# The first set of a second attention in pieces of 4, 4 and 8 tiles, two units spread by TensorE, other load order, new list of the first stages

## The chip, the cores and the metric

The kernel runs on one core of a Trainium2 chip. The metric is the device time of one execution in microseconds (us): the median of three runs of the kernel before is 1481.76 us (1481.65 to 1482.52). The core has five engines with a program of their own each: PE (TensorE, matrix products), DVE (VectorE), ACT (ScalarE), POOL (GpSimd) and SP (SyncE, which here only issues transfers). They wait for each other through semaphores; 16 DMA engines move data.

## The reference

```python
def _attn_ref(x, inducing):           # x: 4 x 12416 x 128, inducing: 32 x 128
    ...
    def mab(q, kv):
        s = scale * (q @ kv.transpose(0, 2, 1))
        s = s - s.max(-1, keepdims=True)
        a = np.exp(s)
        a /= a.sum(-1, keepdims=True) + 1e-09
        return a @ kv
    h = mab(I, x)
    return mab(x, h)

def _moe_ref(x, w_gate, w_val, w_out, rms_g):   # 49664 x 128, d_ff 1536
    rms = np.sqrt(np.mean(x * x, axis=-1, keepdims=True) + 1e-06)
    xn = x / rms * rms_g
    g = xn @ w_gate
    silu = g * (1.0 / (1.0 + np.exp(-g)))
    val = xn @ w_val
    return silu * val @ w_out
```

For each of four batches, 32 inducing rows attend to all 12416 rows of x and give h (32 x 128); then each row of x attends to h. A feed-forward layer with an RMS norm and a SwiGLU follows, row by row. The three weights arrive as 64-bit floats.

## The kernel before

**Tiling.** A batch has 97 tiles of 128 rows, in seven sets: five of 16 tiles, one of 15 and one of 2 (`per`). For the second attention a set is cut into four units, one for each group of 32 partitions (the last set is one unit), so a batch has 25 units, 100 in all. A unit has 512, 480 or 256 rows of x as columns. The output of the second attention is never formed: a unit's normalised weights `a` (32 values for each row, in a high and a low half) are multiplied on TensorE with stacked products of h and the weights (`stacks`, one for gate and one for value). For each of the 12 blocks of 128 hidden columns a unit passes through `gate`, `silu`, `value`, `times_value` (line 751, the product of silu and value on DVE) and a projection by w_out. The projection is either plain (kind P: one 32-bit product, line 807) or split into two or three parts that ACT, POOL and DVE prepare (kinds S and D: two products at lines 795 and 796 and a third at line 807). The list `sorts` names the kind of each of the 1200 blocks.

**Order.** Nothing is scheduled by the chip: every engine runs its instructions in the order in which the kernel issues them. The order is written out by hand in two strings. `ORDER` is the list of the first stages (`first()`), and `program` with `taken` is that of everything after; `banks`, `workers`, `outputs`, `holders` and `picks` say which buffer each step gets.

**First stages.** For batch 0, TensorE turns each set's rows (`t`, line 908; copied out by ACT `a` or DVE `v`, line 914), multiplies them with the inducing rows (`s`), and DVE takes scores and row maxima (`m`, line 920). The sets are in three groups (0, 1, 2), (3, 4), (5, 6), each with its own maximum (`own`, `mB`, `nb`). ACT takes exponentials (`e`, line 945), DVE turns them (`r`, line 354), TensorE sums (`h`, line 953). At the end the three groups are weighed (`by`, line 966), added by `turn_h` (line 972), and `hT` (line 977) is h turned. Then the second attention's first set is done in two halves of 8 tiles, 256 columns each, steps with a `z` in their name: scores (`sc`, line 994), transpose (`T`), row maximum (`rm`), subtraction (`sub`, DVE), exponential (`ex`), transpose (`ta`), product with the gram matrix of h (`sq`), product and sum (`zm`, `sm`), clamp (`mm`), power -1/2 on POOL (`rt`, line 1032), multiplication (`ap`), transpose (`tb`), and the two halves (`hi` on ACT, `lo` on DVE). TensorE spreads unit 0 to all partitions (`sd`, line 1054), ACT copies it (`cp`); units 1 and 2 are gathered by four transfers each on SP (`gather`, line 647).

Between these steps the list puts the rounding of the 64-bit weights, one chunk of 512 columns at a time: `p`, `u`, `g`, `l` on DVE (lines 226, 239, 248, 254), `P`, `U` mostly on ACT (lines 204, 206), `j` on POOL (line 260), `q` on SP. A chunk's raw words are fetched by `fetch_raw` (line 178), five of them ahead, the others when a place comes free. `st` and `low` make the first stacks (lines 485, 488, 492). `w` with a number is that many products of the identity with itself, whose result is not used.

**Loads.** `load_rows` issues the sets on SP in the order 0 to 6: one transfer for each of sets 0 to 4 (line 104), two for set 5, four for set 6 (line 100). One raw chunk is fetched after set 3 and four after set 6. In set 0 the row of partition p and tile t is 16p+t, so its four units interleave with the output rows by partition groups (`of`).

## Time and profile before

| What | us |
|---|---|
| median of three runs | 1481.76 |
| the profiled execution | 1481.53 |
| its span | 1479.7 |
| TensorE busy in the span | 1467.6 |
| first gate starts (after the span's start) | 46.99 |

The profile is one execution. Its views give, for each engine, busy time, the groups of instructions by line, the idle time ahead of an instruction with what ended it (in brackets, behind an arrow), the chain of waits that ended last, and the time from the issue of a transfer to its landing. In the rows of a timeline the first number is the start after the span's start and the second the length of that row's instructions together; x4 says how many instructions one row holds.

### The profile page before, as it was taken

To read this page: it belongs to the slowest core of one execution; us is meant where nothing else is said; L and a number is where in the kernel's file an instruction comes from. 1 tells how busy PE (TensorE), PEld (TensorE's weight loads), DVE (VectorE), ACT (ScalarE), POOL (GpSimd) and SP (SyncE) were. 2 spreads that over 40 slices of the span, in tenths; PEclk is the share of its full clock that TensorE was granted. 3 is DMA by queue.
4 is the path that set the end of the run, shared out by engine and by line. 5 is a ranking of instruction groups with operands and counts; after the bars stand their busy time and mean duration, and the time that the engine had idled before them with its cause. 6 is when DMAs were issued, how large, how long until landed. Compare 5 with 4: busy or idle time off the path is not lost.

```text
span 1479.7 us, 26001 instructions
## 1 busy us (share of the span) xinstructions
PE 1467.6 (99%) x7286; PEld 1102.4 (74%) x7286; DVE 1420.0 (96%) x2469; ACT 1309.5 (88%) x2605; POOL 1378.8 (93%) x1204
## 2 busy tenths in 40 slices
PE   9999999999999999999999999999999999999998
PEld 6566777877777777787777777777778777787787
DVE  6999998999999999999999999899999999999997
ACT  5798889889988898988998988988998989899997
POOL 1499998999999999999999999999989999999998
PEclk9999999999999999999999999999999999999999
DMA  7694324448453231465656321264232122222122
GB/s 286 129 127 94 68 40 92 88 116 128 78 102 73 42 70 32 94 136 103 116 89 117 56 44 29 43 136 107 58 63 45 33 38 38 42 38 42 36 43 35
DMA packets 391712, 116.28 MB, mean 79 GB/s; under 512 B 365584, under 2 KB 370704, under 8 KB 389008
## 3 DMA queue, kind: packets, MB, share of 16 engines
q1 hardware_dynamic: 390976, 114.55, 39.8%
q8 instruction: 58, 0.95, 0.3%
q14 instruction: 86, 0.70, 0.2%
q10 hardware_dynamic: 592, 0.08, 0.0%
HBM read 53.95 MB, written 27.00 MB: 55 GB/s over the span
## 4 chain that ended last, share of the span: by engine, by line
PE 94%; DVE 2%; DMA 1%; issue 1%; ACT 1%; POOL 0%; SPq 0%; DVEq 0%; ACTq 0%; POOLq 0%
PE gv L807 31%; PE gv L709 17%; PE gv L737 17%; PE gv L795 12%; PE gv L796 12%; PE gv L316 3%; PE gv L369 1%; PE gv L908 1%; DMA xn<-in_x_dram 1%; DVE u L751 0%; PE gv L569 0%; DMA xT<-in_x_dram 0%; PE gv L463 0%; DVE o L239 0%; DVE we L248 0%
## 5 line engine op out<-in xcount | busy, mean ns | idle before, releaser
L719 ACT ACTIVATE silu<-gv 128x512 f32<-128x512 f32 (+2 forms) x1200 | 671.4, 592 | 74.4 <-PE gv L709 55.9
L815 POOL TENSOR_TENSOR xn<-xn,xn 128x512 fp32r<-128x512 f32 (+2 forms) x486 | 605.0, 1264 | 15.5 <-PE gv L796 14.0
L709 PE MATMUL gv<-a,sg 128*128 128x512 f32 (+2 forms) x1188 | 482.1, 431 | 0.6 <-DMA a<-lo 0.6
L737 PE MATMUL gv<-a,sv 128*128 128x512 f32 (+2 forms) x1188 | 449.4, 411 | 0.3 <-ACT silu L719 0.2
L751 DVE TENSOR_TENSOR gv<-silu,gv 128x512 f32<-128x512 f32 (+2 forms) x643 | 422.1, 676 | 10.2 <-PE gv L737 5.0
L764 ACT ACTIVATE xn<-gv 128x512 fp32r<-128x512 f32 (+1 forms) x629 | 370.0, 598 | 32.9 <-DVE gv L751 27.0
L751 DVE TENSOR_TENSOR u<-silu,gv 128x512 f32<-128x512 f32 (+2 forms) x557 | 354.5, 652 | 12.2 <-PE gv L737 5.3
L807 PE MATMUL gv<-u,wo 128*128 128x512 f32 (+2 forms) x724 | 353.5, 573 | 1.1 <-DVE u L751 1.0
L770 DVE SCALAR_TENSOR_TENSOR xn<-xn,gv 128x512 fp32r<-128x512 f32 (+1 forms) x516 | 337.4, 664 | 8.9 <-ACT xn L764 6.2
L709 PEld LDWEIGHTS gv<-a,sg 128*128 128x128 f32 x1188 | 223.3, 189 | 106.6 <-issue 32.4
L737 PEld LDWEIGHTS gv<-a,sv 128*128 128x128 f32 x1188 | 222.9, 189 | 86.9 <-issue 21.4
L815 POOL TENSOR_TENSOR xn<-xn 128x512 fp32r<-128x512 f32 (+1 forms) x204 | 255.3, 1257 | 7.0 <-PE gv L796 4.0
L777 POOL TENSOR_TENSOR xn<-u,xn 128x512 fp32r<-128x512 f32 (+2 forms) x174 | 218.2, 1260 | 15.7 <-ACT xn L761 15.2
L815 POOL TENSOR_TENSOR u<-xn,u 128x512 fp32r<-128x512 f32 (+2 forms) x133 | 167.9, 1271 | 2.1 <-PE gv L796 1.9
L795 PE MATMUL gv<-xn,xn 128*128 128x512 f32 (+1 forms) x441 | 169.7, 385 | 0.0
L807 PEld LDWEIGHTS gv<-u,wo 128*128 128x128 f32 x724 | 134.9, 190 | 27.9 <-issue 10.9
L795 PE MATMUL gv<-xn,more 128*128 128x512 f32 (+2 forms) x355 | 137.6, 388 | 0.0
L796 PE MATMUL gv<-xn,xn 128*128 128x512 f32 (+2 forms) x363 | 135.9, 374 | 0.0
L807 PE MATMUL gv<-xn,xn 128*128 128x512 f32 (+2 forms) x363 | 135.0, 383 | 0.5 <-POOL xn L815 0.3
L783 ACT ACTIVATE xn<-xn 128x512 fp32r<-128x512 f32 (+2 forms) x194 | 122.0, 633 | 10.8 <-POOL xn L777 9.2
L761 ACT ACTIVATE xn<-u 128x512 fp32r<-128x512 f32 (+2 forms) x194 | 121.0, 625 | 6.9 <-DVE u L751 6.1
L807 PE MATMUL gv<-xn,more 128*128 128x512 f32 (+2 forms) x311 | 118.8, 396 | 0.0
(223 smaller groups left out, 1787.8 us busy)
## 6 DMA issues: line engine op xcount, KB each, us to landing
out_dram<-o SPq DMA_DIRECT2D x320, 64.0 KB, 2.0
xT<-in_x_dram SPq DMA_DIRECT2D x60, 256.0 KB, 4.6
xn<-in_x_dram SPq DMA_DIRECT2D x60, 256.0 KB, 5.8
a<-hi SPq DMA_DIRECT2D x156, 64.0 KB, 2.0
a<-lo SPq DMA_DIRECT2D x156, 64.0 KB, 2.0
xn<-in_x_dram SPq DMA_DIRECT2D x5, 1024.0 KB, 9.6
xn<-w SPq DMA_DIRECT2D x18, 256.0 KB, 4.2
out_dram<-o SPq DMA_DIRECT2D x64, 60.0 KB, 2.0
```

Of the source, the lines that this page charges most:

```text
L709: nc.tensor.matmul(g[:, 0:T], stacks[b][0][:, ts(j, P)], halves_in_turn(one["a"][:, 0:T]), start=True, stop=True)
L719: nc.scalar.activation(sl[:, 0:T], gates.pop(n)[:, 0:T], AF.Silu)
L737: nc.tensor.matmul(v[:, 0:T], stacks[b][1][:, ts(j, P)], halves_in_turn(one["a"][:, 0:T]), start=True, stop=True)
L751: nc.vector.tensor_tensor(out=to, in0=sl[:, 0:T], in1=v[:, 0:T], op=ALU.mult)
L764: nc.scalar.activation(hi, t["u"], AF.Copy, scale=-(1.0 - 2.0 ** -13) * 2.0 ** -12)
L770: nc.vector.scalar_tensor_tensor(out=t["lo"], in0=t["hi"].bitcast(F32), scalar=4096.0, in1=t["u"], op0=ALU.mult, op1=ALU.add)
L777: nc.gpsimd.tensor_tensor(out=t["lo"], in0=t["u"], in1=t["hi"].bitcast(F32), op=ALU.subtract)
L783: nc.scalar.activation(t["hi"], t["hi"].bitcast(F32), AF.Copy, scale=-(2.0 ** -12))
L795: nc.tensor.matmul(to, weight_of(0, j), halves_in_turn(t["hi"]), start=not one["q"], stop=False)
L796: nc.tensor.matmul(to, weight_of(1, j), halves_in_turn(t["lo"]), start=False, stop=last)
L807: nc.tensor.matmul(to.rearrange("p (n h) -> p h n", h=2) if step2 else to, lhsT, rhs, start=one["left"] == NJ, stop=one["left"] == 1)
L815: nc.gpsimd.tensor_tensor(out=t["lo"], in0=t["hi"].bitcast(F32), in1=t["lo"].bitcast(F32), op=ALU.add)
```

## The change

The load order becomes sets 1, 2, 0, 3 to 6, then all five raw chunks. Set 1 comes in three transfers, set 2 in two, set 5 in two as before. Set 0 is placed in another way, in 12 transfers: tiles 0 to 3 hold rows 0 to 511, tiles 4 to 7 rows 512 to 1023, tiles 8 to 15 the rest, so that unit 0 is piece 0, unit 1 is piece 1, and units 2 and 3 lie in piece 2.

In the list of the first stages, the second attention's set 0 goes in pieces of 4, 4 and 8 tiles. Pieces 0 and 1 run through to the end; TensorE spreads both of their units with eight selecting matrices (`sel`, four quarters by two halves), eight products for a unit, and two copies on ACT for each unit take them out. Piece 2 is taken up to its exponential; its other ten steps stand in `program`. Units 2 and 3 are gathered by eight transfers each. The row maximum is subtracted on POOL for pieces 0 and 1, and `ap1` and `lo1` go to POOL. The share of a group is multiplied in as soon as its sum is there (`hs`), 1/l goes into `fold` (`fr`), and `turn_h` is three separate steps. The copies, warm-ups and rounding steps are put on other engines and into another order, and `low1` stands in the list. The sums of group 1 have a bank of their own.

`banks`, `workers`, `outputs`, `holders`, `sorts`, `picks`, `program` and `taken` are new. `sorts` has 366 blocks of kind P, 191 D and 643 S, where before it had 362, 195 and 643.

```diff
+    PIECES = {1: (slice(0, 4), slice(4, 8), slice(8, 16)), 2: (slice(0, 8), slice(8, 16)), full - 1: (slice(0, 8), slice(8, 15))}
...
-            for part in (slice(0, 8), slice(8, n)) if s == full - 1 else (slice(0, n),):
+            if not s:
+                for k in range(4):
+                    q, tiles, first = (4, slice(4 * k, 4 * k + 4), 0) if k < 2 else (2, slice(8, 16), 2 * (k - 2))
+                    d = xrows[ds(512 * k, 512), :].rearrange("(i q t) c -> q i t c", i=m, q=q)
+                    for e in range(q):
+                        nc.sync.dma_start(out=t[ts(first + e, m), tiles, :], in_=d[e])
+                return
+            for part in PIECES.get(s, (slice(0, n),)):
                 nc.sync.dma_start(out=t[:, part, :], in_=d[:, part, :])
...
+        if (b, s) == (0, 0):
+            a = moving[b, u] = xnp.tile([P, 512], F32R, name="xn1") if u == 2 else astk.tile([P, 512], F32R, name="a")
+            for k, half in enumerate((hi, lo, hi, lo)):
+                for e in range(2):
+                    nc.sync.dma_start(out=a[ts(k, m), ts(e, w // 2)].bitcast(F32),
+                                      in_=half[ts(2 * (u - 2) + e, m), w // 2:w].bitcast(F32))
+            return
...
-    for s in range(NS):
+    for s in (1, 2, 0, *range(3, NS)):
         load_rows(0, s)
-        for _ in range(1 if s == 3 else 4 if s == NS - 1 else 0):
+        for _ in range(5 if s == NS - 1 else 0):
             fetch_raw(*unread.pop(0))
...
-        open w3 t02 t00 t03 v00 t01 a01 a03 v02 t10 a10 t12 t13 s0 a12 a13 t11 t20 t21 a20 t23 m0 a23 t22 a22 a21 v11
-        s1 t32 m1 t30 s2 a32 t33 t31 p00 P00 v30 u00 m2 own0 g00 Uv00 mB0 t40 l00 j00 q00 t42 nb0 a31 a33 t41 a40 v42 e0 t43
...
-        r6 h6 l10 j10 q10 by0 by1 by2 P20 g20 u11 turn_h hT sc0z sc1z U20 l20 j20 q20 T0z rm0z sub0z ex0z T1z gram ta0z w7 sq0z rm1z
-        sub1z ex1z zm0z ta1z sm0z st1 sq1z mm0z zm1z P11 silu sm1z mm1z rt0z rt1z p01 st0 U11 ap0z low0 tb0z
-        ap1z hi0z tb1z lo0z w12 sd0z hi1z P01 cp0z lo1z w1 sd1z u01 cp1z w3 gather1 gather2
+        open w4 t10 t11 c11A w2 t13 c13A c10V t12 t20 t21 c21V c12A s1 m1 c20A t22 t23 t00 c00A c22V t01 t02 t03 c23V
+        c01V c02A s2 c03A s0 m2 m0 t31 own0 t30 c31A c30V t33 mB0 nb0 c33V t32 c32V e2 t42 c42A r2 t40 t43 c40V t41 c41V
+        e0 t50 c43A s3 r0 s4 m3 e1 ls0 c50A p00 m4 t60 c60A p10 t53 c53A own1 t52 c52A r1 t51 mB1 nb1 u10 c51A s6 m6 p20
+        h0 u00 e3 r3 s5 m5 e4 ls1 h1 own2 mB2 P00A g00 nb2 U00A l00 j00 least P20A e6 h3 r4 e5 ls2 r6 h2 share shared h4
+        P10A hs0A r5 tl spl u20 p11 h5 U10A rl g20 hs1A g10 frA th0 l10 U20A h6 hs2A l20 P11A th1 th2 hgV hTA w2 sc0 sqh
+        gc sc1 j10 T0 rm0 sub0G sc2 st0 ex0 T1 rm1 sub1G T2 ta0 q00 j20 rm2 ex1 sq0 ta1 zm0 sm0 mm0V w1 sq1 stc0 q10 st1
+        stc1 rt0 zm1 sm1 mm1V sub2V ex2 ap0V tb0 low0 hi0 rt1 ap1G lo0V w6 sdh0 sdl0 silu p01 tb1 u01 hi1 cpa0A u11 sdm0
+        cpb0A low1 P01A lo1G sdh1 sdm1 U11V cpb1A q20 sdl1 cpa1A U01V
...
+        PARTS = (slice(0, 4), slice(4, 8), slice(8, 16))
...
+        def select(u, q, kind):
+            half = split_of[0, 0][kind][:, both(u)[0]]
+            T.matmul(at["spread", u, q // 2][:, ts(q % 2, P)], sel[q, kind], half, start=not kind, stop=bool(kind))
+
+        def spread(u):
+            for k in range(2):
+                at["spread", u, k] = bank()
+                select(u, 2 * k, 0)
+
+        def spread_rest(u, k):
+            select(u, 2 * k, 1)
+            select(u, 2 * k + 1, 0)
+            select(u, 2 * k + 1, 1)
...
+            for name, (engine, step) in piece.items():
+                add(0, engine, step, call=(), key=("piece", 0, name))
```

In the list, a letter behind a name is the engine (A for ACT, V for DVE, G for POOL); `sdh` is `spread`, `sdl` and `sdm` are `spread_rest` for the two halves of a unit's columns.

More of the change, by code (lines that the diff above doesn't have):

```diff
@@ L1051, in spread @@
-        def spread(k):
-            ps = at["spread", k] = bank()[:, 0:HT * m]
-            for n, half in enumerate(split_of[0, 0]):
-                T.matmul(ps, sel[:, n, :, :].rearrange("p k m -> p (k m)"), half[:, both(k)[0]], start=not n, stop=bool(n))
-        def spread_copy(k):
-            if not k:
-                moving[0, 0] = astk.tile([P, 512], F32R, name="a")
-            S.copy(out=moving[0, 0][:, both(k)[0]], in_=at.pop(("spread", k)))
+                split_of[0, 0] = [halves.tile([P, 512], F32R, name="hi")]
@@ L1065, in first, with choice @@
         do = {"open": f["open_"], "least": least_of, "share": shares, "shared": shared,
-              "fold": f["fold_l"], "turn_h": turn_h, "hT": copy_h, "gram": lambda: (f["square_h"](), f["copy_gram"]()), "silu": table}
+              "tl": f["total_l"], "spl": f["spread_l"], "rl": f["inverse_l"], "sqh": f["square_h"], "gc": f["copy_gram"],
+              "silu": table}
+        def choice(name, step):
+            for letter, by in engine.items():
+                do[name + letter] = lambda by=by: step(by)
+        choice("fr", fold_r)
+        choice("hT", copy_h)
+        choice("hg", scale_h)
         for n in range(1, 40):
@@ L1096, in first @@
+        for u in range(2):
+            do[f"sdh{u}"] = lambda u=u: spread(u)
+            for k, name in enumerate(("sdl", "sdm")):
+                do[f"{name}{u}"] = lambda u=u, k=k: spread_rest(u, k)
+            for k, name in enumerate(("cpa", "cpb")):
+                choice(f"{name}{u}", lambda by, u=u, k=k: spread_copy(by, u, k))
         for name in ORDER.split():
             do[name]()
+        assert not turns and not works and not outs
+        for engine_name, name, step, *args in (("DVE", "ta", turn_a), ("PE", "sq", square), ("DVE", "zm", times),
+                                               ("DVE", "sm", total), ("POOL", "mm", clamp, G), ("POOL", "rt", root),
+                                               ("POOL", "ap", apply, G), ("DVE", "tb", turn_b), ("ACT", "hi", upper),
+                                               ("POOL", "lo", lower, G)):
+            piece[name] = (engine_name, lambda step=step, args=args: step(*args, 2))
```

609 lines of the change are left out of this document (315 added, 294 removed), and 62 rows, old and new, of the table taken.

## The prediction

> **What bounds the kernel now.** I read the page first, then busy time by stretch, then TensorE's waits, then the chain and the queues of the first 50 us.
>
> ```profile
> PE 1467.6 (99%) x7286; PEld 1102.4 (74%) x7286; DVE 1420.0 (96%) x2469; ACT 1309.5 (88%) x2605; POOL 1378.8 (93%) x1204
> ...
> PE 94%; DVE 2%; DMA 1%; issue 1%; ACT 1%; POOL 0%; SPq 0%; DVEq 0%; ACTq 0%; POOLq 0%
> ...
> 30.00:40.00 10.00, 8.21 (x110) 5.80 (x102) 8.52 (x25) 3.08 (x11) 2.54 (x2) 1.00 0.42 134
> ...
> 200.00:300.00 100.00, 100.00 (x576) 77.12 (x578) 93.78 (x158) 93.49 (x176) 94.09 (x77) 1.00 0.38 77
> ...
> PE gv L807 <- DVE u L751: 1.0, 2, 0.7
> PE gv L709 <- DMA a<-lo: 0.6, 1, 0.6
> PE gv L807 <- POOL xn L815: 0.3, 1, 0.3
> PE gv L737 <- ACT silu L719: 0.2, 1, 0.2
> ```
>
> The first two rows are the page's busy times and its chain by engine; the next two are stretches (length, busy us of PE, PEld, DVE, ACT, POOL, then clock and DMA); the last four are all of TensorE's waits after 47 us, 2.1 us in 1430. TensorE is the bound from the first gate to the end, at a granted clock of 1.00. So the time is: when the first gate starts, plus TensorE's work after it, plus some 2 us of waits, plus a tail. Only these four can change. A DVE at 96% does not set the end, but it decides how soon the first products reach TensorE.
>
> ```profile
> 34.99 1.07 PE L994 MATMUL gv<-xT,hT 128*32 128x256 f32 x16 [0.65 <-DVE hT L977]
> ...
> 46.99 0.48 PE L709 MATMUL gv<-a,sg 128*128 128x512 f32 x1
> ...
> 46.68 0.69 DVE L248 SCALAR_TENSOR_TENSOR we<-sg,we 128x512 int32<-128x512 int32 x1
> ...
> 51.42 1.88 DVE L751 TENSOR_TENSOR u<-silu,gv 128x512 f32<-128x512 f32 x3
> ```
>
> These rows of the timeline (start, length) are the landmarks: the second attention's first scores at 34.99, the first gate at 46.99, the first product at 51.42. The third is one of the rounding steps that DVE runs ahead of that product.
>
> **The change part by part.**
>
> *1. Loads.* Set 0 now comes third and in 12 transfers, set 1 in 3, set 2 in 2; all five weight chunks go last.
>
> ```profile
> 4.72 0.47 SPq L104 DMA_DIRECT2D xn<-in_x_dram  x1
> ...
> 6.32 0.34 SPq L100 DMA_DIRECT2D xn<-in_x_dram  x1
> 8.76 0.32 SPq L100 DMA_DIRECT2D xn<-in_x_dram  x1
> ...
> 15.01 0.35 SPq L178 DMA_DIRECT2D sc<-in_moe_w_val_dram  x1
> ...
> sc<-in_moe_w_val_dram SPq DMA_DIRECT2D x1, 512.0 KB, 8.5
> ...
> 4.98 1.65 PE L152 MATMUL gv<-ident 128*128 128x128 f32 x6
> ...
> 8.88 1.50 PE L908 MATMUL gv<-ident,xn 128*128 128x128 f32 x12 [0.21 <-DMA xn<-in_x_dram]
> ...
> 36.23 1.81 PE L152 MATMUL gv<-ident 128*128 128x128 f32 x14
> ...
> 32.75 1.05 DVE L966 TENSOR_SCALAR u<-gv,nb,rl 128x128 f32<-128x128 f32 x3 [0.34 <-PE gv L953]
> ...
> L412 ACT ACTIVATE hg<-gv,columns 128x128 f32<-128x128 f32 x3 | 1.2, 400 | 0.0
> ...
> L408 ACT COPY hT<-gv 128x128 f32<-128x128 f32 x3 | 0.9, 289 | 0.0
> ```
>
> In SP's timeline, eight loads leave by 5.2 us; the ninth leaves at 6.32, the next one 2.4 us later, which is one 1 MB set: SP has eight loads under way and waits for the one eight before. Now those eight are 2.2 MB instead of 6.9 (five pieces of sets 1 and 2, three of set 0), and set 3, the 18th, waits for the tenth. At 1 MB in 2.4 to 2.5 us, an opening delay of 3.9 us (6.32 less 2.44) and a reissue near 11.5 us, I estimate set 3 at 15.5 us and the first weight chunk, behind 6.2 MB of rows, at 22 to 23.5. In the old order the second chunk, at the same count of bytes plus one chunk, was there at 15.01+8.5=23.5. DVE's p00 would be reached near 22.5, so it costs 0 to 1 us; I take 0.6, bounds 0 and 3 (everything queued on DVE behind p00 and p10, own_max of group 1 among it, waits too).
> TensorE can't start sooner: it opens behind the identity products, and there are three warm-ups more (w4 and w2 against w3). Six rows took 1.44 us to the next start, so 0.24 a row, two rows a warm-up: +1.4 at that rate, +0.8 at the 14 rows that took 1.81 at 36 us; I take +0.9. Of that 0.6 comes back: the wait of 0.21 for set 1, which now comes first, and as much again twice, an estimate, as copies and transposes move between DVE and ACT.
> Between the last sum, which released the weighings at 32.75, and the first scores at 34.99 the old list has three weighings (1.05 us), six products and two rounding steps of DVE ahead of the copy: 2.3 us. Now two of three weighings and products are done earlier, and rl goes into fold. Left: a weighing and a copy on ACT, 0.4 and 0.29 by the last two rows (mean ns of one), two products 0.4, hops 0.5: 1.6 us, a gain of 0.7.
> Sum of stage one: +0.6 +0.9 -0.6 -0.7 = **+0.2 us** (bounds -1.2 and +2.8). The first scores start at 35.2.
>
> *2. From the first scores to the first gate*, 46.99-34.99 = 12.0 us now, on halves of 256 columns; now quarters of 128 for units 0 and 1, with the subtraction on POOL.
>
> ```profile
> 35.69 0.45 DVE L998 STREAM_TRANSPOSE sc<-gv 128x256 f32<-128x256 f32 x1 [0.16 <-PE gv L994]
> ...
> L354 DVE STREAM_TRANSPOSE hT<-sc 128x64 f32<-128x64 f32 x3 | 0.7, 234 | 0.0
> ...
> L670 ACT ACTIVATE more<-more 128x128 fp32r<-128x128 f32 x1 | 0.3, 310 | 0.0
> ...
> 76.39 0.46 POOL L668 TENSOR_TENSOR more<-wo,more 128x128 fp32r<-128x128 f32 x1
> ...
> 40.62 3.28 POOL L1032 TENSOR_TENSOR rs<-ms,rt 128x8 f32<-128x8 f32 x2 [3.73 <-DVE ms L1029]
> ...
> L603 POOL TENSOR_TENSOR rs<-rs,rt 128x16 f32<-128x16 f32 x3 | 0.7, 225 | 0.4 <-ACT rt L600 0.4
> ...
> 45.91 0.36 PE L1054 MATMUL gv<-hi,u 128*128 128x256 f32 x1
> ...
> 46.14 0.38 PE L1054 MATMUL gv<-lo,u 128*128 128x256 f32 x1
> ```
>
> A DVE step of 128 columns lies between 0.23 (64) and 0.45 (256): 0.30. ACT 0.31, POOL 0.46. The power takes 1.64 for 8 columns where a product of 16 takes 0.23; if that scales, 4 columns take 0.9, if it is fixed, 1.64. I take 0.9, since 8 columns cost 1.4 more than a product, which looks like work per element; the other end stays in the range. First piece to its power: scores 0.5, transpose and maximum 0.6, subtraction 0.46, exponential 0.31, transpose 0.3, product with gram 0.55 with its hop, times and sum 0.6, clamp 0.17, hops 0.5: 4.0. TensorE's list puts all of unit 1's spread before the first gate, so the rest runs over the second piece: two powers 1.8, multiplication on POOL 0.46, transpose 0.3, ACT 0.31, subtraction on POOL 0.46, six selections at 0.22 (the start-to-start of the last two rows) 1.3, hops 0.6: 5.2. Together **9.2 us, so -2.8** (bounds -3.8, where unit 1's steps overlap better, and -1.3 with the power fixed).
> The Trainium skill has a rule against this part: "SBUF — State Buffer", Who interferes with whom, says that a VectorE instruction in a two-port mode, or with two SBUF inputs, and a GpSimd instruction that reads SBUF exclude each other for the whole instruction. By it the three POOL steps could each wait for one 0.3 to 0.6 us VectorE step, about 1 us in all, and this part would give -1.8; the old trace has no such pair on this path, so it shows neither.
>
> *3. TensorE's work after the first gate.* The list of kinds has 366 plain projections for 362.
>
> ```profile
> 76.94 0.22 PE gv L795
> 77.15 0.22 PE gv L796
> ...
> 78.45 0.86 PE gv L807 x2
> ...
> 40.06 0.70 PE L1017 MATMUL gv<-eT,gram 128*128 128x256 f32 x2
> ```
>
> In the chain a split block has three passes of 0.22 us (two at L795 and L796, the third at L807 with the same width), a plain one 0.86: 0.21 more at 512 columns. By width: one more of 512, five more of 480, two fewer of 256, 2400 columns, **+1.0 us**. The third piece (8 tiles) leaves its gram product behind the first gate: 256 columns, half of 0.86, **+0.44**. Its other nine steps go to DVE, ACT and POOL under plain projections; DVE's 1.6 us of it cost nothing while a plain block holds TensorE for 1.29 us and DVE for 0.62, and up to 1.6 if DVE is the late one.
>
> *4. Waits after the first gate.* The 0.6 for unit 1's gather goes, as TensorE spreads that unit. Of the 1.0 for products, about half goes: stack_low of the values is now in the first list, where before DVE ran six rounding steps ahead of it; now five steps, at most 0.69 each by the row at 46.68, stand before the first product, so it follows the first gate by some 3 us instead of 4.4. **-1.0** (bounds -1.5 and +1.5, DVE's third piece being the loss).
>
> *5. The tail* has the same steps. 0.
>
> Sum: +0.2 -2.8 +1.0 +0.4 -1.0 = -2.2 us. The profiled execution took 1481.53 us (span 1479.7), 0.23 under the median of three; 1481.53-2.2 = **1479.3 us**.
>
> **The rivals.**
>
> *A, more is gained.* Chunks arrive in time (+0.2 becomes -1.0), and the second piece runs wholly beside the first (-3.8): the sum is -4.4, **1477.1**. For it: DVE is busy 8.52 of 10 in 30:40, so it has slack to use, ACT 3.08. Against it: the eight-deep queue.
>
> *B, nothing is gained.* The power is a fixed 1.64 (+1.5) and POOL's steps wait 0.7 more: -2.2+2.2 = 0, **1481.5**. For it: no power of another width in the trace. "It doesn't do what it says" falls in here: the first gate is earlier, but the first product, for which DVE must still do five rounding steps, is where it was.
>
> *C, slower: the gathers of units 2 and 3.* These two units now need the third piece, and 8 transfers each instead of 4.
>
> ```profile
> 49.44 1.28 POOL L260 TENSOR_TENSOR xn<-o,we 128x512 f32<-128x512 f32 x1 [5.55 <-PE gv L709]
> ...
> 74.46 5.75 SPq L111 DMA_DIRECT2D xT<-in_x_dram  x5
> 80.88 1.06 SPq L647 DMA_DIRECT2D a<-hi  x1
> 81.99 0.58 SPq L647 DMA_DIRECT2D a<-lo  x1
> ...
> a<-hi SPq DMA_DIRECT2D x156, 64.0 KB, 2.0
> ```
>
> Between the first gate and unit 2's first, the list has 48 gates and values, 19 plain projections, four stacks, six scores and little else: 48x0.215+19x0.86+4x0.86+5.3+1.9 = 37 us. That gate comes near 82. POOL must first do six joins and four whole splits at 1.28, six splits of 128 or 256 columns at 0.46 to 0.75 and the piece's four steps (1.64 for the power, about 1.7 for the rest), 12.8+3.3+3.3 = 19.4 us from about 46, with waits for DVE's steps between, so the piece is ready at 70 to 74; 8 issues at 0.6 and 2.0 to land make 77 to 81. Slack is 1 to 5 us, and SP was once held 5.75 us by five row loads at this very place. Held so for unit 2 with a slack of 1, TensorE stops 4.7 us, and unit 3, 8 transfers behind, 2 to 3 more: -2.2+7.4 = +5.2, **1486.7**. It decides from a delay of SP or POOL beyond slack plus 2.2 us. Against it: SP's work between is mostly under way by then.
>
> **How the numbers follow.** Forecast 43%, A 28%, B 12%, C 17%. About 0.2% (3.0 us) is what a measurement of this kernel can tell from no change, and 1481.76-3.0 is 1478.8, half a us under my forecast; of the forecast's 43 points 18 lie below it. Faster: 18+28 = 46%; same: 25+11+2 = 38%; slower: C's 15 and 1 of B, 16%. The likeliest case's own range is 1477.6 to 1481 (stage one's and the chain's bounds). A takes the lower end to 1476.4; the upper one, with a late chunk (+2.6) or the milder half of C, is 1484.
>
> **What would show it.** The first gate at 44.4 (43 to 46) instead of 46.99; the first scores at 35.2; the first weight chunk landing at 22 to 23.5 and DVE idle before p00 by under 1 us; powers of 4 columns at 0.9 us; TensorE's waits after the first gate about 1 us, none at unit 2's first gate for a DMA; 366 plain projections. I am wrong if the first scores come after 37.5, if the first product doesn't move by 3 us or more, or if TensorE waits over 2 us for a gather.

## The result, and the profile after

| | before | after |
|---|---|---|
| median, us | 1481.70 (6 runs, 1481.37 to 1482.52) | 1487.55 (6 runs, 1484.07 to 1488.87) |
| profiled execution, its span | 1481.53, 1479.7 | 1487.66, 1485.9 |
| first scores start | 34.99 | 39.56 |
| first gate starts | 46.99 | 48.49 |
| first gate to the end of the span | 1432.7 | 1437.4 |

The ratio is 1.0036 (95% interval 1.0025 to 1.0048): the change makes the kernel slower, by 5.9 us. Run again later beside other kernels it took 1484.47 (11 runs), 1.0018 (1.0009 to 1.0027) of the kernel before. Its runs scatter over 4.8 us, those of before over 1.2; why is not shown for this kernel (the last section has what the clock explains in others).

The page of the changed kernel: busy times, and the chain by engine. TensorE is busy 1.3 us less than before in a span 6.2 us longer.

```profile
PE 1466.3 (99%) x7282; PEld 1102.6 (74%) x7282; DVE 1422.0 (96%) x2473; ACT 1305.4 (88%) x2603; POOL 1372.4 (92%) x1209
...
PE 94%; DMA 2%; DVE 2%; ACT 1%; SPq 0%; issue 0%; POOL 0%; ACTq 0%; DVEq 0%
```

The landmarks in its timeline: DVE's step p10, the first scores, the first gate.

```profile
28.49 0.43 DVE L239 TENSOR_SCALAR we<-sc 128x512 int32<-128x512 int32 x1 [0.40 <-DMA sc<-in_moe_w_val_dram]
...
39.56 0.43 PE L1032 MATMUL gv<-xT,hT 128*32 128x128 f32 x8 [0.29 <-ACT hT L927]
...
48.49 0.65 PE L717 MATMUL gv<-a,sg 128*128 128x512 f32 x2
```

Three stages: up to the first scores 4.57 us were lost, from there to the first gate 12.00-8.93 = 3.07 were gained, and from the first gate on 4.70 were lost.

**The first loss is in the loads.** The first part of the chain of waits (start, length), then SyncE's timeline:

```profile
2.58 8.88 DMA xn<-in_x_dram
14.18 8.43 DMA xn<-in_x_dram
22.62 5.84 DMA sc<-in_moe_w_val_dram
```

```profile
0.72 2.31 SPq L112 DMA_DIRECT2D xn<-in_x_dram  x5
3.06 10.60 SPq L109 DMA_DIRECT2D xn<-in_x_dram  x12
13.70 2.43 SPq L112 DMA_DIRECT2D xn<-in_x_dram  x4
16.18 1.91 SPq L101 DMA_DIRECT2D xn<-in_x_dram  x4
19.28 0.35 SPq L191 DMA_DIRECT2D sc<-in_moe_w_gate_dram  x1
22.62 0.35 SPq L191 DMA_DIRECT2D sc<-in_moe_w_val_dram  x1
```

The twelve issues of set 0 take 10.6 us: from the ninth load on, each waits for the load eight places before it. The 13th waits for the second half of set 2, which lands at 11.46 (first row of the chain). Set 3 goes out at 13.70, and the words for p10 at 22.62. Stretches of five us, before and then after (length; busy PE, PEld, DVE, ACT, POOL; clock, DMA share, GB/s):

```profile
5.00:10.00 5.00, 4.79 (x33) 4.58 (x33) 1.48 (x3) 1.29 (x3) 0.00 (x0) 1.00 1.01 424
10.00:15.00 5.00, 5.00 (x43) 2.99 (x42) 1.53 (x4) 3.40 (x7) 0.00 (x0) 1.00 1.01 423
```

```profile
5.00:10.00 5.00, 4.31 (x36) 4.07 (x37) 0.88 (x2) 1.76 (x4) 0.00 (x0) 1.00 0.98 322
10.00:15.00 5.00, 3.55 (x27) 1.92 (x25) 3.37 (x6) 1.07 (x2) 0.00 (x0) 1.00 0.61 161
```

Two faults in the two rows of the changed kernel: from 5 to 10 us the DMA is about as busy as before (0.98) and moves a quarter less, and from 10 to 15 it is not even busy (0.61).

**The second loss is at unit 4.** TensorE's waits behind the start of the second attention, then its timeline there, and two stretches, before and after:

```profile
PE gv L717 <- DMA a<-lo: 2.7, 1, 2.7
PE gv L815 <- DVE u L759: 0.9, 1, 0.9
PE gv L803 <- ACT xn L791: 0.8, 1, 0.8
...
PE gv L745 <- ACT silu L727: 0.4, 1, 0.4
```

```profile
118.50 0.38 PE L804 MATMUL gv<-xn,more 128*128 128x512 f32 x1
121.62 1.19 PE L717 MATMUL gv<-a,sg 128*128 128x512 f32 x2 [2.74 <-DMA a<-lo]
122.60 0.63 PE L815 MATMUL gv<-xn,xn 128*128 128x512 f32 x1
123.03 0.63 PE L745 MATMUL gv<-a,sv 128*128 128x512 f32 x1
```

```profile
110.00:130.00 20.00, 20.00 (x100) 12.48 (x92) 19.70 (x35) 16.68 (x33) 17.37 (x16) 1.00 0.51 94
```

```profile
110.00:130.00 20.00, 16.39 (x80) 9.84 (x79) 15.59 (x29) 13.39 (x26) 13.46 (x11) 0.91 0.67 125
```

TensorE stands 2.74 us for unit 4's gather. Behind that its matmuls start 0.43 us apart (122.60, 123.03) where 0.22 is usual: the granted clock is 0.5 for 3.4 us, hence 0.91 over the stretch. In these 20 us TensorE is idle for 3.6 us, 2.74 of them for the gather and 0.80 for ACT's part of a split projection, and half clock for 3.4 us costs 1.7 more. That is more than the 4.70 lost behind the first gate; what the stall costs net is measured with e2 below.

Why the gather is late stands in SyncE's timeline, with POOL's row that makes its source:

```profile
100.07 4.61 SPq L877 DMA_DIRECT2D out_dram<-o  x4
104.73 7.14 SPq L119 DMA_DIRECT2D xT<-in_x_dram  x7
111.99 2.81 SPq L559 DMA_DIRECT2D xn<-xn  x2
114.90 2.63 SPq L877 DMA_DIRECT2D out_dram<-o  x4
117.62 0.57 SPq L655 DMA_DIRECT2D a<-hi  x1
```

```profile
111.91 1.27 POOL L637 TENSOR_TENSOR lo<-aT,hi 128x512 fp32r<-128x512 f32 x1 [2.24 <-ACT hi L633]
```

The source is ready at 113.18. SyncE comes to the gather only at 117.62: its rows have followed each other without a pause for 20 us. In the kernel before the same gather left 4.35 us earlier:

```profile
113.27 1.28 SPq L647 DMA_DIRECT2D a<-hi  x1
```

### The profile page after: what moved, and what is told of

It is laid out like the page before. It is cut to its first block, busy times and chain, and to the rows that moved or that the text cites. A ratio compares the mean times of both kernels' runs of the same rounds, so it can differ in the third digit from the quotient of the medians.

```text
span 1485.9 us, 26008 instructions
## 1 busy us (share of the span) xinstructions
PE 1466.3 (99%) x7282; PEld 1102.6 (74%) x7282; DVE 1422.0 (96%) x2473; ACT 1305.4 (88%) x2603; POOL 1372.4 (92%) x1209
## 4 chain that ended last, share of the span: by engine, by line
PE 94%; DMA 2%; DVE 2%; ACT 1%; SPq 0%; issue 0%; POOL 0%; ACTq 0%; DVEq 0%
PE gv L815 31%; PE gv L717 17%; PE gv L745 17%; PE gv L803 12%; PE gv L804 12%; PE gv L324 2%; PE gv L377 1%; DMA xn<-in_x_dram 1%; PE gv L571 1%; DMA sc<-in_moe_w_val_dram 0%; PE gv L465 0%; ACT silu L727 0%; DMA xn<-xn 0%; DVE u L759 0%; PE gv L487 0%
## 5 line engine op out<-in xcount | busy, mean ns | idle before, releaser
L823 POOL TENSOR_TENSOR xn<-xn,xn 128x512 fp32r<-128x512 f32 (+2 forms) x454 | 562.6, 1254 | 21.2 <-PE gv L804 16.1
L717 PE MATMUL gv<-a,sg 128*128 128x512 f32 (+2 forms) x1188 | 477.0, 432 | 2.9 <-DMA a<-lo 2.7
L772 ACT ACTIVATE xn<-gv 128x512 fp32r<-128x512 f32 (+2 forms) x614 | 359.7, 599 | 30.4 <-DVE gv L759 23.6
L815 PE MATMUL gv<-u,wo 128*128 128x512 f32 (+2 forms) x732 | 358.3, 574 | 0.9 <-DVE u L759 0.9
L778 DVE SCALAR_TENSOR_TENSOR xn<-xn,gv 128x512 fp32r<-128x512 f32 (+2 forms) x505 | 329.1, 663 | 8.3 <-ACT xn L772 5.6
L823 POOL TENSOR_TENSOR xn<-xn 128x512 fp32r<-128x512 f32 (+2 forms) x214 | 267.1, 1256 | 4.0 <-PE gv L804 3.3
L785 POOL TENSOR_TENSOR xn<-u,xn 128x512 fp32r<-128x512 f32 (+2 forms) x163 | 201.8, 1242 | 18.2 <-ACT xn L769 13.1
L803 PE MATMUL gv<-xn,xn 128*128 128x512 f32 (+2 forms) x444 | 171.4, 386 | 0.8 <-ACT xn L791 0.8
L804 PE MATMUL gv<-xn,xn 128*128 128x512 f32 (+2 forms) x371 | 138.6, 374 | 0.5 <-DVE xn L778 0.5
L815 PE MATMUL gv<-xn,xn 128*128 128x512 f32 (+2 forms) x371 | 138.3, 383 | 0.0
L803 PE MATMUL gv<-xn,more 128*128 128x512 f32 (+2 forms) x337 | 129.2, 383 | 0.0
L815 PE MATMUL gv<-xn,more 128*128 128x512 f32 (+2 forms) x281 | 110.0, 399 | 0.0
```

Source lines behind the costliest of these rows:

```text
L717: nc.tensor.matmul(g[:, 0:T], stacks[b][0][:, ts(j, P)], halves_in_turn(one["a"][:, 0:T]), start=True, stop=True)
L772: nc.scalar.activation(hi, t["u"], AF.Copy, scale=-(1.0 - 2.0 ** -13) * 2.0 ** -12)
L778: nc.vector.scalar_tensor_tensor(out=t["lo"], in0=t["hi"].bitcast(F32), scalar=4096.0, in1=t["u"], op0=ALU.mult, op1=ALU.add)
L785: nc.gpsimd.tensor_tensor(out=t["lo"], in0=t["u"], in1=t["hi"].bitcast(F32), op=ALU.subtract)
L803: nc.tensor.matmul(to, weight_of(0, j), halves_in_turn(t["hi"]), start=not one["q"], stop=False)
L804: nc.tensor.matmul(to, weight_of(1, j), halves_in_turn(t["lo"]), start=False, stop=last)
```

## The experiments

Each is the changed kernel with the edit shown, five rounds beside the kernel before. The table has, from the timelines: DVE's start of p10, the first scores, the first gate, the issue of unit 4's gather, TensorE's wait for it; then the median (5 to 11 runs) and the ratio to the kernel before with its interval. "After" in the first row is the profile above.

| run | p10 | scores | gate | gather | wait | us | ratio |
|---|---|---|---|---|---|---|---|
| after | 28.49 | 39.56 | 48.49 | 117.62 | 2.7 | 1487.55 | 1.0036 (1.0025-1.0048) |
| e1 | 26.61 | 37.68 | 46.61 | 115.17 | 2.5 | 1482.79 | 1.0007 (0.9999-1.0016) |
| e2 | 27.88 | 38.95 | 47.88 | 112.45 | 0 | 1482.52 | 1.0008 (0.9999-1.0017) |
| e3 | 26.80 | 37.86 | 46.79 | 112.74 | 0 | 1481.80 | 1.0000 (0.9991-1.0009) |
| e4 | 26.10 | 37.16 | 46.09 | 113.66 | 2.4 | 1482.34 | 1.0007 (0.9998-1.0016) |
| e5 | 28.28 | 39.34 | 48.27 | 116.18 | 2.7 | 1484.47 | 1.0018 (1.0009-1.0027) |
| e6 | 27.30 | 38.36 | 47.28 | 111.34 | 0 | 1480.25 | 0.9992 (0.9984-1.0001) |
| e7 | 28.18 | 39.24 | 48.17 | 117.66 | 0 | 1485.44 | 1.0026 (1.0015-1.0037) |
| e8 | 29.82 | 40.88 | 49.80 | 118.54 | 1.7 | 1489.05 | 1.0049 (1.0036-1.0061) |
| e9 | 27.96 | 39.03 | 47.95 | 114.85 | 2.2 | 1484.84 | 1.0023 (1.0014-1.0032) |
| e10 | 32.23 | 43.30 | 52.52 | 120.38 | 2.6 | 1487.98 | 1.0049 (1.0037-1.0062) |
| e11 | 25.99 | 37.06 | 45.99 | 110.92 | 0 | 1481.92 | 1.0005 (0.9997-1.0014) |
| e12 | 28.68 | 39.75 | 48.67 | 112.55 | 0 | 1481.47 | 1.0003 (0.9994-1.0012) |
| e13 | 23.88 | 34.95 | 44.00 | 110.49 | 2.0 | 1479.20 | 0.9982 (0.9973-0.9991) |
| e14 | 23.55 | 34.61 | 43.54 | 107.65 | 0 | 1477.89 | 0.9976 (0.9968-0.9985) |
| e15 | 26.56 | 37.62 | 46.96 | 110.80 | 0 | 1481.26 | 0.9999 (0.9990-1.0008) |
| e16 | 28.30 | 39.35 | 48.28 | 115.95 | 2.5 | 1483.70 | 1.0014 (1.0006-1.0023) |
| e17 | 26.51 | 37.57 | 46.50 | 111.34 | 0 | 1482.22 | 1.0004 (0.9996-1.0013) |
| e18 | 25.89 | 36.96 | 46.28 | 109.76 | 0 | 1480.73 | 0.9991 (0.9982-1.0000) |

The rows share one regularity: in all of them the first scores start 11.05 to 11.07 us behind p10, and in 15 of 19 the first gate 8.92 or 8.93 behind those (9.05 to 9.34 in e10, e13, e15 and e18, where the clock falls there). From p10 to the first gate the new list takes 20.0 us in these 15, and up to 20.4 in the other four. What varies at the start is mainly when p10 begins.

### The two suspects, alone and together

```diff
e1, e3
-                        nc.sync.dma_start(out=t[ts(first + e, m), tiles, :], in_=d[e])
+                        (nc.scalar if k < 2 else nc.sync).dma_start(out=t[ts(first + e, m), tiles, :], in_=d[e])
e2, e3: in program the store O of unit 1 moved behind unit 4's gather
-   vpTds.pOsm.v.vhv.gmrepmsnhga.q
+   vpTds.psm.v.vhv.gmrepmsnhgaO.q
```

> The changed kernel with one edit: the eight 64 KB transfers of set 0 go out on ScalarE's DMA queue, the four of 128 KB and all else stay on SyncE's. Theory Q (the queue of SyncE): set 3 left at 13.70 us only because it is the 18th load of a queue that has eight under way and the ninth waits for the one eight before; now it is the 10th and leaves by 7 us, the DMA has no hole at 9 to 13 us, the first weight chunk goes out by 15 and p10's words land by 24 instead of 28.46; first scores at 35 to 36.5 instead of 39.56, first gate at 44 to 45.6 instead of 48.65, time 1483 to 1484.5. Rival W (the new list of the first stages itself is longer: warm-ups, copies on ScalarE, order): the loads come sooner, but the first scores stay at 38 to 39.6 and the time at 1486.5 to 1487.5. Rival B (the DMA is full in any case, 6.2 MB of rows stand ahead of the chunks): the hole closes elsewhere, the chunks land within 1 us of now, time as now.

p10 is 1.9 us earlier, under half of what was expected of theory Q; the rivals W and B both fall, as the scores move with the words. The rows tell why no more (SyncE's queue, then ScalarE's):

```profile
0.72 5.05 SPq L112 DMA_DIRECT2D xn<-in_x_dram  x5
8.03 2.38 SPq L109 DMA_DIRECT2D xn<-in_x_dram  x4
```

```profile
1.18 7.00 ACTq L109 DMA_DIRECT2D xn<-in_x_dram  x8
```

ScalarE's eight issues take 7.0 us together and SyncE's next load leaves at 8.03. The limit of eight is not one queue's: it holds for the program's loads over both queues.

> The changed kernel with one edit: the store of unit 1 (four transfers) is issued behind the gather of unit 4 instead of ahead of it. Theory S (SyncE is late): the gather goes out at about 114.9 instead of 117.62 and lands near 118.8, TensorE's wait of 2.74 us for it falls below 0.5, and the granted clock of 0.5 over 3.4 us right behind it, which cost 1.7 us, is gone with it: 4 to 4.5 us less, 1483 to 1483.6. Rival H (the half clock is a throttle that comes whatever the wait): only the wait goes, 2.5 to 2.8 us less, 1484.8 to 1485.1, the clock row of 0.5 still there. Rival V (the gather waits for VectorE's or GpSimd's lower halves of set 1, or the store is wanted as soon): nothing changes, or a store's buffer is late later, 1487 to 1488.

SyncE's timeline:

```profile
112.45 0.54 SPq L655 DMA_DIRECT2D a<-hi  x1
```

The gather leaves 5.2 us sooner than in the changed kernel (3.7 sooner than in e5), no wait for it is left, and the clock is 1.00 throughout that stretch: the span is 1480.3, 5.6 under the changed kernel's, 0.6 of it from an earlier first gate. So theory S: here the half clock comes with the wait and goes with it. Against the changed kernel run again (e5) the median is 2.0 lower. The net price of the stall shows when the starts of the 1200 silu steps are set against those of e2: between 108 and 131 us the changed kernel falls from 0.93 to 4.54 us behind, so 3.6, and e5 from 0.48 to 3.22, so 2.7; e5 keeps that distance to the end. The changed kernel loses 1.1 more between 182 and 427 us, which e5 does not.

> Both edits: the eight small loads of set 0 on ScalarE's queue and the store of unit 1 behind the gather of unit 4. Theories Q and S together: 1478.5 to 1480.5, that is 1.2 to 3.2 us below the kernel before, with the first gate at 44 to 45.6 and no clock row of 0.5. If the two disturb each other (an earlier first gate brings unit 4's gate earlier, while SyncE is as late as before), the stall at unit 4 comes back by up to the 3 to 4 us that the start gained: 1482 to 1484.

1481.80: level with the kernel before, 1.3 us over the upper end of what was expected; the first gate came at 46.79, not at 45.6 or less. The stall did not come back.

### Fewer or other transfers at the start

```diff
e4: sets 1 and 2 in one transfer each
-    PIECES = {1: (slice(0, 4), slice(4, 8), slice(8, 16)), 2: (slice(0, 8), slice(8, 16)), full - 1: (slice(0, 8), slice(8, 15))}
+    PIECES = {full - 1: (slice(0, 8), slice(8, 15))}
e8
-        for _ in range(5 if s == NS - 1 else 0):
+        for _ in range(2 if s == 3 else 3 if s == NS - 1 else 0):
```

> The changed kernel with sets 1 and 2 in one transfer each instead of three and two. Theory Q: set 3 becomes the 15th load and waits for the 7th, a small one of set 0, instead of the 10th; but the 10th load still waits for set 2, now 1 MB in one transfer, so that the queue still stands at 8 to 11 us; set 3 leaves 0.5 to 3 us earlier than 13.70, TensorE starts 0.5 to 1.5 us later, the first scores come at 38 to 40 and the time is 1486 to 1488.5. Rival W: the first scores follow TensorE's later start alone, 40 to 41, time 1488 to 1489.

p10 came 2.4 us earlier, more than theory Q said, and W is out: the first scores moved down with p10, not up.

> The changed kernel as it is, beside the next three. Theory: 1486.5 to 1488, its words for p10 landing near 28.5 and the first scores 11.1 us behind that landing, as in all four runs so far (28.46 and 39.56; 26.59 and 37.68; 26.77 and 37.86; 26.08 and 37.16). Rival (the five us that every edit so far seemed to bring are a difference of chips or of the hour): 1482 to 1484, so that the two edits of the loads bring less than 2 us.

p10, the first scores and the first gate repeat within 0.3 us; unit 4's gather comes 1.4 earlier, with the same wait for it. The median does not repeat: it lies above the rival's range and below the theory's. So of the five us that e1 to e4 seem to gain on 1487.55, some three need not be theirs. The kernel before moved by 0.6 us at most between the five series (1481.08 to 1481.68). The series ran on different chips, e5 to e8 on another than e1 to e4, so chip and hour are not told apart. Medians are set against e5's 1484.47 from here on, and steps of the start against the landmarks, which hold.

> The changed kernel with the first two weight chunks loaded right behind set 3 and three behind set 6. Theory P (the first scores come 11.1 us behind p10's words): the words land at 23 to 25, DVE reaches p00 and p10 without a wait, but sets 4 to 6 land 2.6 us later, so the scores follow the sets: 38.5 to 40.5 (the bound moves from the words to the sets) if the sets are the limit, or 34.5 to 36.5 if the words alone are. Rival W (the list itself is long): 39.3 to 40 whatever lands when.

The words came sooner and p10 later (29.82): now it waits for what the sets release. Bringing one load forward only puts off another.

```diff
e6: e1, e2 and e4 together
e11: e2 and e4, set 0 in 8 transfers (tiles 0 to 7 of a partition block in one), and
-    for s in (1, 2, 0, *range(3, NS)):
+    for s in (1, 2, 3, 0, *range(4, NS)):
e9: the 8 transfers alone; e10: the order alone
```

> The changed kernel with three edits: sets 1 and 2 whole, the eight small transfers of set 0 on ScalarE's queue, the store of unit 1 behind the gather of unit 4. Theory Q: SyncE then has two loads, four of set 0 and set 3 among its first eight, so set 3 leaves by 4 us, p10's words land at 23.5 to 25, the first scores come at 34.6 to 36.1, the first gate at 43.7 to 45.2, no wait for unit 4: 1478 to 1479.5. Rival B (the DMA is full): p10's words land at 25.5 to 26.5 as in the runs with one of the edits, time 1480.5 to 1481.8.

p10 at 27.30, no earlier than with whole sets alone, and 1480.25: nearer to rival B. Two queues share the eight, so set 3 did not leave early.

> The changed kernel with set 0 in 8 transfers of 128 KB instead of 12 (the first two pieces of a quarter go in one transfer). Theory N (the program has eight loads under way over all queues, in its own order: a load goes out when the eighth before it has landed): set 3 becomes the 14th and waits for an early one; it leaves when set 2's second half lands, 11.5 instead of 13.70, so everything behind it is some 2 us earlier: p10's words at 26 to 27, first scores at 37.1 to 38.1, 1.2 to 2.2 us less than the changed kernel run again (39.34, 1484.47), 1482.3 to 1483.3. Rival B (bytes alone): set 3 leaves earlier, but the words land within 0.5 us of 28.3 and the time stays at 1484 to 1485.

The theory that the count of loads does it all falls here, with one row of e9's stretches:

```profile
10.00:15.00 5.00, 3.51 (x30) 2.23 (x28) 2.68 (x5) 0.58 (x1) 0.00 (x0) 1.00 0.97 217
```

The hole is closed (share 0.97 instead of 0.61), yet 217 GB/s come through where the kernel before has 423 at a share of 1.01, and p10 gains 0.3 us. The transfers in flight there are mostly those of set 0, to 32 partitions each. Smaller packets are not the reason: in the trace of e9 packets of 4 KB to 128 partitions (sets 1 and 2, 4 to 8 us) took 159 ns in the median, set 0's of the same size (from 12.1 us on) 266. The Trainium skill, "SBUF — State Buffer", section Door 1: The DMA port swizzle, has the rule: 32 partitions reach 8 of the 16 ports, so half of the bandwidth. The rate in e9 agrees, 217 for 423.

> The changed kernel with set 3 loaded ahead of set 0. Theory N: a whole megabyte more is under way while the small transfers take their turns, set 3 leaves by 3.5 us and the hole at 9 to 13 us closes; set 0 is complete near 15 to 16 us as before (15.3), p10's words land at 25.5 to 27, first scores 11.1 us behind them, 36.6 to 38.1, time 1481.7 to 1483.2. Rival T (TensorE's own list wants set 0 ahead of set 3): set 0 comes 2 us later, TensorE waits that long more for it and the first scores stay at 39 to 40.

Set 0 came so late that TensorE stopped twice for it. Its waits for rows up to 40 us, and the stretch from 10 to 25 us, with a clock of 0.66:

```profile
PE gv L942 <- DMA xn<-in_x_dram: 5.7, 2, 3.4
...
10.00:25.00 15.00, 9.30 (x52) 4.72 (x50) 3.98 (x8) 2.40 (x5) 0.00 (x0) 0.66 0.79 256
```

In the changed kernel these waits come to 4.7 us in five. Set 0's last tiles are turned from 20.18 us on instead of 16.39, and the clock, at half from 14.35 to 24.59 us, adds to it. That is rival T, and p10 at 32.23 is the worst of all.

> Four edits: set 0 in 8 transfers, sets 1 and 2 whole, set 3 ahead of set 0, the store of unit 1 behind the gather of unit 4. Theory N: 4 MB of rows under way from the start, p10's words land at 24 to 25.5, first scores at 35.1 to 36.6, first gate at 44 to 45.6, no wait for unit 4: 1477.8 to 1479.6, under the kernel before by 1.8 to 3.6. Rival T: set 0 late, first scores at 38 or later, 1480 to 1481.

Beside whole sets the order shows no cost: p10 at 25.99, where e4 had 26.10, and half a us later than expected. The profiled run took 1479.34, as expected, but the median is 1481.92. The three longest runs (1483.08 to 1483.58) have a mean clock of 0.996 or 0.997 where the shortest has 0.999, and 0.002 of 1480 us is 3 us; where the clock fell in them was not traced.

### Set 0 in one transfer

```diff
e13, e14
-                for k in range(4):
...
-                        nc.sync.dma_start(out=t[ts(first + e, m), tiles, :], in_=d[e])
+                nc.sync.dma_start(out=t[:], in_=d)
e16: the 12 transfers, blocks in the order 0, 2, 1, 3
```

In e13 and e14 the rows of set 0 are not where the output needs them.

> The changed kernel with set 0 loaded in one transfer of 1 MB over all 128 partitions, as in the kernel before; its rows then stand in other places, so the spreading of set 0 over units is left out. Theory H (a transfer to 32 partitions moves half the bytes of one to 128 while the DMA is full, and eight small loads do not fill it): 0.82 MB per 2 us from 4 to 18 us, no hole, set 3 leaves by 6.5, p10 starts on VectorE at 24 to 25.3, first scores 11.07 us behind it at 35.1 to 36.4, first gate 8.93 us behind these at 44.0 to 45.3; the stall at unit 4 stays at 1 to 2.7 us; 1480 to 1481.5. Rival W (the first list itself is longer than forecast): p10 after 26.5 and first gate after 46.5, 1482 to 1484.

Its SyncE (set 3 is the first of the four at L108), one stretch, and TensorE's landmarks:

```profile
3.74 2.80 SPq L108 DMA_DIRECT2D xn<-in_x_dram  x4
7.51 5.60 SPq L101 DMA_DIRECT2D xn<-in_x_dram  x4
```

```profile
10.00:15.00 5.00, 4.04 (x36) 2.78 (x36) 3.27 (x6) 1.26 (x4) 0.00 (x0) 1.00 1.00 424
```

```profile
34.95 0.43 PE L1028 MATMUL gv<-xT,hT 128*32 128x128 f32 x8 [0.29 <-ACT hT L923]
...
44.00 0.74 PE L713 MATMUL gv<-a,sg 128*128 128x512 f32 x1
```

Set 3 leaves at 3.74, the DMA moves 424 GB/s as in the kernel before, and p10 starts at 23.88 and the first gate at 44.00. Set 0's twelve transfers are the whole of the late start, 4.3 us against e5.

> Set 0 in one transfer (as in the run with that label) and the store of unit 1 behind the gather of unit 4. If the loads of set 0 and the order on SyncE are the whole miss of the forecast: first gate at 44.0 to 45.3, no wait for unit 4, no clock row of 0.5 behind it, 1477.3 to 1479.3, 2 to 4 us below the kernel before. If a third cause is left: 1480 or more.

Both faults away: 1477.89, 3.5 us below the kernel before, inside the first of the two ranges. No third cause is needed.

> The changed kernel with the 12 transfers of set 0 in another order: partition blocks 0, 2, 1, 3 instead of 0, 1, 2, 3, so that two transfers that follow each other go to the two halves of the partitions. Theory H with ports (a block of 32 and its neighbour in the same half of 64 share their way in): packets of 2 KB to set 0 take under 115 ns and those of 4 KB under 190 in place of 117 to 135 and 213 to 230, p10 is 0.3 to 1 us earlier than in the changed kernel run again (28.28), time 1483.5 to 1484.3. Theory without ports (any transfer to 32 partitions is slow, or only the count): p10 within 0.2 us of 28.3.

p10 at 28.30: the order of the blocks changes nothing. Set 0's packets did not become shorter either: those of 2 KB took 120 ns in the mean (121 in e5), those of 4 KB 215 (207). That transfers to 32 partitions run at half the rate rests on the rate and the packets of e9; that two of them side by side go faster did not show.

### Why SyncE is late at unit 4

```diff
e12: the second eight tiles of units 2 and 3 left out, the first eight taken twice
-                for e in range(2):
-                    nc.sync.dma_start(out=a[ts(k, m), ts(e, w // 2)].bitcast(F32),
-                                      in_=half[ts(2 * (u - 2) + e, m), w // 2:w].bitcast(F32))
+                nc.sync.dma_start(out=a[ts(k, m), 0:w].rearrange("i (e c) -> i e c", e=2).bitcast(F32),
+                                  in_=half[ts(2 * (u - 2), m), w // 2:w].bitcast(F32).unsqueeze(1).to_broadcast((m, 2, w // 2)))
e7: (nc.scalar if u == 3 else nc.sync).dma_start for the eight of unit 3
```

> The changed kernel with the eight transfers of unit 3's gather on ScalarE's queue. Theory G (the twelve more transfers of the gathers of units 2 and 3 put SyncE 5 to 6 us behind, and that alone makes unit 4's gather late): SyncE is 5 us earlier from 92 on, unit 4's gather goes out by 114, the 2.7 us wait and the half clock vanish, 3.5 to 4.5 us less than the changed kernel, unless ScalarE, held by eight issues, lets TensorE wait for a silu (up to 2 us given back). Rival O (the order of store and gather is what does it, SyncE waits there for the lower halves of set 1 in any case): the wait stays above 1.5 us and the half clock stays.

This could not decide: ScalarE's eight issues took 5.4 us (89.77 to 95.16), and TensorE stood for a silu long before unit 4. Its longest wait behind 43 us:

```profile
PE gv L745 <- ACT silu L727: 5.0, 2, 4.3
```

> The changed kernel, with units 2 and 3 gathered in 4 transfers each instead of 8, of the same bytes; for that the second eight tiles of each are left out and the first eight taken twice. Theory G (the number of those transfers puts SyncE behind): SyncE is 4 to 6 us earlier from 98 us on, unit 4's gather leaves by 114.2 where the lower halves of set 1 are done, TensorE's wait for it is under 0.6 us and the granted clock stays at 1.0: 3.5 to 4.5 us less than the changed kernel. Rival O (the order of store and gather alone): the gather still leaves after 116, wait above 1.5 us, the clock row of 0.5 still there.

SyncE's timeline:

```profile
109.83 2.62 SPq L876 DMA_DIRECT2D out_dram<-o  x4
112.55 0.57 SPq L654 DMA_DIRECT2D a<-hi  x1
```

With the store still ahead of it the gather leaves at 112.55, 5.1 us earlier than in the changed kernel and 3.6 earlier than in e5, though the first gate is as late as there, and no wait for it is left. Theory G: the number of transfers for units 2 and 3 puts SyncE behind. Moving the store (e2) takes the wait away without removing this cause.

### Versions with every row in its place

```diff
e15: e2 and e4
e17: e2, and for set 0
+                nc.sync.dma_start(out=t[:, 8:16, :], in_=xrows[ds(1024, 1024), :].rearrange("(p t) c -> p t c", p=P))
...     (its units 2 and 3 are then stored in 8 transfers each)
e18: e17 and e4
```

> The changed kernel with sets 1 and 2 in one transfer each and the store of unit 1 behind the gather of unit 4, everything on SyncE and nothing left out. From the runs with one of the edits: first gate near 46.1 (its own run), no wait at unit 4 (2.4 and 1.7 us less): 1477.8 to 1479.5 in the profiled run, 1479 to 1480.5 in the median, below the kernel before by 0.6 to 2 us. Rival: the earlier units make SyncE late again, 1481 to 1482.

1481.26, at its rival's: p10 came at 26.56 where e4 had 26.10, and the clock fell ahead of the first gate.

> The changed kernel with the second half of set 0 (tiles 8 to 15) in one transfer over 128 partitions, the rows of units 2 and 3 dealt out so that it is in order, their stores in 8 transfers each instead of 4, and the store of unit 1 behind the gather of unit 4. Theory H: 0.5 MB less at half rate is 0.6 us of DMA time, and the 15th load instead of the 18th is set 3; p10 at 26.3 to 27.3 (28.28 without), first gate at 46.3 to 47.3, no wait at unit 4: 1479 to 1480.3. Rival S (SyncE has no room for eight more stores at 115 to 135): a wait of 1 to 3 us at unit 5 or 6, 1481 to 1483.5.

p10, the first gate and the missing wait are theory H's, the time is not (1482.22). No wait at unit 5 or 6 came, so it is not rival S. By the starts of the 1200 silu steps its profiled run is 1.5 us ahead of e2 at 147 us, level with it at 306 and 1.1 behind at 1142, with no wait of TensorE between 147 and 306 us; why is open.

> The same with sets 1 and 2 in one transfer each. Theory H: set 3 is the 12th load, p10 at 25 to 26, first gate at 45 to 46: 1478 to 1479.5, below the kernel before by 2 to 3.4. Rival S as above, 1480 to 1482.

p10 as expected, the first gate 0.3 late by the clock, 1480.73.

e6 (1480.25) and e18 (1480.73) lie about 1 us under the kernel before, with intervals that end at 1.0001 and 1.0000: better than the change by far, not surely better than the old kernel. The 3.5 us of e14 were not reached with all rows in place: a store of a unit laid out over 128 partitions would by count need 16 transfers in place of 4, and at 0.66 us an issue (2.63 for four) that is an estimated 8 us more of SyncE's time for each unit. It was not tried.

## Why the prediction was wrong

The forecast was 1479.3, -2.2 us; measured was +5.9 in the median and +6.1 in the profiled run. By its steps:

1. **Loads, +0.2: this step failed, by 4.4 us.** "I estimate set 3 at 15.5 us and the first weight chunk ... at 22 to 23.5." The rule of eight loads under way was right. But the eight were priced "at 1 MB in 2.4 to 2.5 us", the rate of whole sets over 128 partitions. Set 3 landed at 19.28 (the gate chunk leaves when it has), the gate chunk's p00 started at 27.06, p10 at 28.49. The term for p00, "I take 0.6, bounds 0 and 3", stood for the whole delay, and it had neither the half rate of transfers to 32 partitions nor the hole that small transfers leave among eight under way. The rest of the step was sound in sum: in e13, without the twelve transfers, the first scores came at 34.95, a forecast 35.2.
2. **Scores to first gate, 12.0 to 9.2: right.** 8.93. The two 4-column powers take 1.01 and 1.04 us in the trace, not 0.9, and the other steps overlapped a little better. The exclusion of DVE and POOL that would have made it 10.2 did not show in the sum.
3. **TensorE's work, +1.44, and 4. waits, -1.0:** together +0.44 forecast. The term missing in step 4 is the stall at unit 4, net 3.6 us (2.7 in e5). Without it, in e2, first gate to end is 1432.4 us, 0.3 under the kernel before. That this is near the forecast is luck, for both parts were off. TensorE's busy time behind the first gate is 1425.0 us in e2 and 1425.3 before, so the work did not grow by 1.44, though it has the 366 plain projections; why not is open (the profile models the ends of products). And nothing was saved on waits: the named ones are 2.5 us in e2 where before had 2.1, the largest of them again for the first product.
5. **Rival C** was near the cause, at the wrong place. It counted the eight gather transfers for each of units 2 and 3 as time of SyncE, but priced the wait at units 2 and 3 themselves. They were in time; the work queued behind them was not, and it was unit 4's gather that came late. The prediction looked at who needs those transfers, not at who stands behind them. That its 1486.7 is near the result is chance: it is a forecast start with a large stall, and measured was a late start with a smaller one.

All three signs of being wrong came: the first scores after 37.5, a wait over 2 us for a gather, and the first product, which did not move 3 us earlier but 0.6 later, to 52.01. It follows the first gate by 3.5 us, so step 4's "some 3 us" was close; only the gate was late.

```profile
52.01 1.88 DVE L759 TENSOR_TENSOR u<-silu,gv 128x512 f32<-128x512 f32 x3
```

With both faults removed (e14) the first gate is at 43.54 and the time 1477.89, in the likeliest case's own range of 1477.6 to 1481: the sum forecast for the new list holds, though not each of its terms; what its loads and gathers cost was not seen.

## What to carry to other kernels

Price a load by the partitions that it reaches and by its place among the loads under way, not by its bytes: here one megabyte in twelve transfers made the start 4.3 us later than in one. When a step is given more transfers, follow the issuing queue on until it has a pause, and look at the first thing behind that is needed in time. And find the one early step from which all the rest follows at a fixed distance (here p10, 20.0 us ahead of the first gate): it turns many experiments into one number.

## What the hardware showed beside this

**The clock falls in fixed windows.** In each trace all changes of the granted clock lie on a grid of 3.413 us: in the changed kernel it fell 34 times 3.413 us behind the first entry at full clock and rose one step later. Taken over all runs, a window of the first 150 us that began at full clock and in which TensorE was idle for 1.97 us or more was followed by a window at half clock in all nine cases (1.97 to 2.69 us); behind windows with 1.84 us or less there was none, but for the five named below. So e10's wait of 2.64 us, which falls across the edge of two windows, cost no clock, and e13's of 2.0 us, inside one, was followed by 3.4 us at half clock. The Trainium skill, "TensorE: Matmul & The Clock Gate", Part 1, gives a free-running window of 3413 ns, which agrees; there the Trainium skill, under "Why this matters for your kernels", asks for no gaps over some 3 us, and here 2.0 us were enough. Five runs (e10, e13, e14, e15, e18) also fell to half clock close to the first gate, from 0.9 us ahead of it to 0.3 behind, after a window with 0.63 to 0.72 us idle; why is open. In e8, e10 and e11 the longer runs are those with the lower mean clock (e8: 1486.32 us at 1.000, 1491.18 at 0.996). In the changed kernel's own six they are not: the shortest and the longest both have 0.997.

**The eight loads under way belong to the program, not to a queue** (e1): a second queue gave no ninth.

**DMA issues on ScalarE are not free**: eight took 5.4 us of its time at 90 us (e7), and TensorE waited 4.3 us for it.
